# A scheduler's counts for a transpose through DRAM, and an SBUF margin 64 bytes wider, in a two-MoE kernel

## The chip, the cores and the metric

One core of a Trainium2 chip runs the whole program: TensorE (PE, with its weight loads shown apart as PEld), VectorE (DVE), ScalarE (ACT), GpSimd (POOL) and SyncE (SP), which here issues the transfers. The metric is the device time of one execution in microseconds, median of three. Less is better.

## The reference

Pooled attention, then an ELU mixture layer, then a second mixture layer with a softmax-gated linear unit and a layer norm. The change concerns the last of them:

```python
def _moe2_ref(x, w_in, w_out, g_ln):          # x: 4608 x 512, d_ff = 1024
    h = x @ w_in
    e = np.exp(h - np.max(h, axis=-1, keepdims=True))
    solu = h * (e / (np.sum(e, axis=-1, keepdims=True) + 1e-09))
    mu = np.mean(solu, axis=-1, keepdims=True)
    var = np.mean((solu - mu) ** 2, axis=-1, keepdims=True)
    ln = (solu - mu) / np.sqrt(var + 1e-06) * g_ln
    return (ln @ w_out).astype(np.float32)
```

## The kernel before

Attention and the first MoE fill the first 877 us of the execution. The second MoE follows. It works on 36 tiles of 128 tokens, in 18 pairs `n`; `tiles_of(n)` gives a pair's two tiles, called A (the first) and B (the second) here.

**The products of a pair.** `x @ w_in` is done by seven products P1, P2, S2, S1, S3, T4, S4 (`z_mul`, `prod`, L1008 to L1042), each of six matmuls with 512 columns. Numbers are split into a high and a low part. Seven weight tiles of 8192 bytes per partition are the moving operands. Three of them, B11 (product P1), B21 (P2) and T1 (S1), are written in place into the pool `pm` at SBUF's right edge. The other four, T2 (S2), T3 (S3), T4 (T4) and B22 (S4), are fetched from DRAM into the ring `w` of the pool `sb` on the left. In the compiled program of before, the `pm` tiles begin at bytes 204736, 212928 and 221120 of a partition, each 64 past a multiple of 128. The `sb` tiles (33536, 25344, 74496, 66304) begin on multiples of 128. The pool `edge`, one tile of 8 floats that nothing reads, lies to the right of `pm`. The scratch pool `pg` lies to the left of `pm`.

**The banks and their copies.** P1, S2, S3 and T4 add up in one bank X. ScalarE copies the bank out between them (`snap`, L1025: `p1` after P1, `u2` after S2, `u3` after S3). So S2 waits for the copy `p1`, with only P2 between, and S3 waits for `u2`, with only S1 between.

**A tile's way.** When its `h` stands: maximum (`max`, DVE L1066), exponential (`exp`, ACT L1072), product (`mul`, DVE L1076 to L1079), mean taken off (`sub`, ACT L1083), square (`sq`, ACT L1088), variance (`var`). Then the tile is transposed. In the first and the last pair TensorE does it (`pe`). In the other 16 pairs, 32 tiles, the tile goes through DRAM: a 32 by 32 transpose on DVE (`T`, L1102), a store to `zd` (`s`, L1107), four loads back into `dT` (`l`, L1114), the high part on ACT (`hi2`, L1122) and the low part on DVE (`lo2`, L1126). Then come 24 matmuls (`po`, L1153), the scaling on ACT (`st`, L1159) and the output store (L1160).

**The order.** TensorE's order is written out (`seq`): in a pair n, P1 P2 S2 S1 S3, then `po` of tile B of pair n-2, then T4 S4, then `po` of tile A of pair n-1. The orders on ACT, DVE and SP come from `arrange`, a list scheduler that runs when the program is built. Each operation has an engine, a duration `dur`, a latency `lat` after it, and dependencies. Working back from TensorE's wanted times it gives each operation a latest start. Going forward, it takes for each engine, among the operations that its own counts say are ready within 0.35 us of the first, the one with the earliest latest start. The engines then execute that order strictly. An operation whose data are late holds up all that stands behind it on its engine. SP also issues the loads of `x1r` (`xl`, L958, 1 MB for two pairs).

Of the kernel before, what the change touches and what calls it, by code (L numbers as in the profile page):

```python
# [8 lines left out]
F32 = mybir.dt.float32  # L9
# [11 lines left out]
def kernel(  # L21
# [16 lines left out]
    P = 128  # L38
# [63 lines left out]
    st = {}  # L102
# [1350 lines left out]
    for pr in range(NTP):  # L1453
# [11 lines left out]
        if last:  # L1465
            third.close()
            att.close()
            edge = ctx.enter_context(tc.tile_pool(name="edge", bufs=1, side="right"))
            edge.tile([P, 8], F32, name="edge")
            pm = ctx.enter_context(tc.tile_pool(name="pm", bufs=3, side="right", reuse_waits="tile"))  # L1470
            att2 = ExitStack()
            pg = att2.enter_context(tc.tile_pool(name="pg", bufs=2, side="right", reuse_waits="tile"))
# [35 lines left out]
        for s in range(7):  # L1508
            banks = o_banks(s)
            for t in range(4):  # L1510
                mul_o(s, t, banks, s in (0, 1, 2), s in (1, 5, 6))
                if s + 1 < 7:
                    for i in range(2):
                        w_ring(("o", s + 1, 2 * t + i))
                    n = ORDER[s + 1]
# [47 lines left out]
    def tiles_of(n):  # L1563

        c, q = divmod(n, 2)
        return 4 * c + q + 2, 4 * c + q
# [87 lines left out]
    tiles = [i for n in range(NPAIR) for i in tiles_of(n)]  # L1654
    outs = [i for key, i in seq if key == "po"]

    def op(key, eng, dur, deps, f=None, *a, lat=0.0, at=0.0):
        ops[key] = dict(eng=eng, dur=dur, deps=deps, lat=lat, at=at, f=f, a=a)
# [3 lines left out]
    for key, n in seq:  # L1662
        k = (key, n)
        if key == "po":
            j = outs.index(n)
# [17 lines left out]
    for n, (a, b) in enumerate(map(tiles_of, range(NPAIR))):  # L1683
        if n > 1:
            c = n // 2
            if n % 2 == 0 and c > 1:
                old = [(k, 2 * c - 3) for k in ("sums", "h0", "hi", "l0", "lo")] if c > 2 else []
                op(("xl", c), "SP", 0.55, old, p2_load, c, lat=5.0, at=20.0 if c == 2 else 0.0)
            x = [("xl", c) if c > 1 else "x1", ("S4", n - 2)]
            op(("open", n), None, 0.0, x, p2_open, n)  # L1690
            op(("sums", n), "DVE", 1.45, [("open", n), ("lo", n - 2), ("hi", n - 2)], p2_sums, n)
            op(("h0", n), "ACT", 0.95, [("open", n)], p2_hi, n, slice(0, 2))
            op(("hi", n), "ACT", 1.02, [("sums", n)], p2_hi, n, slice(2, 3))
            op(("l0", n), "DVE", 1.0, [("h0", n)], p2_lo, n, slice(0, 2))
            op(("lo", n), "DVE", 1.18, [("hi", n)], p2_lo, n, slice(2, 3))
        ha = ("s" if n > 2 else "sub", B_(max(n - 2, 0)) if n > 1 else None)
        hb = ("s" if n > 2 else "mul", A_(n - 1) if n > 2 else A_(0) if n == 2 else None)
        op(("p1", n), "ACT", 0.56, [("P1", n), ("ha0", n - 1)], snap, n, "p1", "X")
        op(("u2", n), "ACT", 0.56, [("S2", n), ("hb1", n - 1)], snap, n, "u2", "X")
        op(("u3", n), "ACT", 0.56, [("S3", n), ("ha0", n), ("ha1", n - 1)], snap, n, "u3", "X")  # L1700
        op(("ha0", n), "DVE", 0.62, [("P2", n), ("p1", n), ha], z_add, n, "ha0")
        op(("hb1", n), "DVE", 0.66, [("S1", n), ("u3", n), hb], z_add, n, "hb1")
        op(("hb0", n), "ACT", 0.57, [("T4", n), ("hb1", n)], z_add, n, "hb0")
        op(("ha1", n), "DVE", 0.66, [("S4", n), ("u2", n), ("ha0", n)], z_add, n, "ha1")
        for i, h, key in ((a, ("hb0", n), "b"), (b, ("ha1", n), "a")):
            j, jo = tiles.index(i), outs.index(i)
            e2 = [(k, tiles[j - 2]) for k in ("T", "pe", "sq")] if j > 1 else []
            op(("max", i), "DVE", 1.18, [h, ("hb1", n)] + ([("st", tiles[j - 6])] if j > 5 else []), s_max, i, n, key)
            op(("exp", i), "ACT", 1.3, [("max", i)] + e2, s_exp, i)
            op(("mul", i), "DVE", 1.75, [("exp", i)], s_mul, i)  # L1710
            op(("sub", i), "ACT", 1.12, [("mul", i)], s_sub, i)
            op(("sq", i), "ACT", 1.2, [("sub", i)], s_sq, i)
            op(("var", i), "DVE", 0.12, [("sq", i)], s_var, i, lat=0.9)
            free3 = [("po", outs[jo - 3])] if jo > 2 else []
            if n in (0, last):
                op(("hi2", i), "ACT", 1.08, [("pe", i)] + free3, t_ph, i)
                op(("lo2", i), "DVE", 1.3, [("hi2", i)], t_pl, i)
            else:
                op(("T", i), "DVE", 1.18, [("sub", i)], t_dve, i)
                op(("s", i), "SP", 0.4, [("T", i)], t_store, i, lat=2.4)  # L1720
                op(("l", i), "SP", 1.75, [("s", i)] + ([("lo2", tiles[j - 2])] if n > 1 else []), t_load, i, lat=2.1)
                op(("hi2", i), "ACT", 1.0, [("l", i)] + free3, t_hi, i)
                op(("lo2", i), "DVE", 1.2, [("hi2", i)], t_lo, i)
            op(("st", i), "ACT", 0.66, [("po", i), ("var", i)] + ([("os", outs[jo - 1])] if jo else []), z_store, i)
            op(("os", i), None, 0.0, [("st", i)], lat=2.4)
    for o in ops.values():
        o["deps"] = [d for d in o["deps"] if d in ops]
    with tc.manual_schedule():
# [38 lines left out]
```

## Time and profile before

| | us |
|---|---|
| median of 3 runs (1273.32 to 1275.31) | 1273.57 |
| profiled execution: its time | 1271.55 |
| profiled execution: span of the trace | 1269.4 |
| TensorE busy in the span | 1242.0 (98%) |
| VectorE / ScalarE busy | 984.8 (78%) / 824.0 (65%) |
| second MoE: first matmul to last | 877.1 to 1265.2 |

The busy shares are averages over three different stages. In a row of a timeline the first number is the start in us, the second the length, then engine, line, operation, tiles written and read, count, and in brackets the idle time just before it and what ended it. "sn" is the tile of the copies p1, u2 and u3, "zX" the bank X.

### The profile page before, as it was taken

Reading aid. Unit: us, or ns where it says so; the run is one execution under the profiler, and the core shown is the slowest. Engines: PE = TensorE matmul, PEld = TensorE weight load, DVE = VectorE, ACT = ScalarE, POOL = GpSimd, SP = SyncE. Lnnn points to the kernel's source line nnn. Section 1 sums busy time; section 2 is a strip of 40 time slices with the busy share of each in tenths; the row PEclk is TensorE's granted clock in tenths of the full one; section 3 lists DMA queues with packets and bytes.
Section 4 is the critical chain, followed back from the end, with each engine's and each line's share of the span. In section 5 each row is a group of like instructions: output and inputs, shape, how many; then the busy total and the mean of one; then the engine's idle time right before and its main releaser. Section 6 shows DMA issues by size and latency. Waiting matters only on the chain.

```text
span 1269.4 us, 17238 instructions
## 1 busy us (share of the span) xinstructions
PE 1242.0 (98%) x5768; PEld 993.9 (78%) x5768; DVE 984.8 (78%) x1484; ACT 824.0 (65%) x1405; POOL 177.7 (14%) x148
## 2 busy tenths in 40 slices
PE   8899999999999999999999999999998999999998
PEld 6777877777777878778888778888886878887777
DVE  8898687978877799676795778986886777778673
ACT  7887566666757784457764468743776667667564
POOL 4564222333210000100000000000000000000000
PEclk8999999999999999999999999999998999999999
DMA  9975366675768867787666888878454544544341
GB/s 323 296 218 191 125 220 221 214 234 168 237 205 274 252 214 243 222 294 199 203 215 201 287 254 270 288 256 306 151 172 141 158 140 143 169 147 141 108 143 57
DMA packets 177065, 263.30 MB, mean 207 GB/s; under 512 B 16465, under 2 KB 96849, under 8 KB 175953
## 3 DMA queue, kind: packets, MB, share of 16 engines
q1 hardware_dynamic: 176976, 262.21, 64.5%
q8 instruction: 46, 0.75, 0.2%
q14 instruction: 43, 0.34, 0.1%
HBM read 182.46 MB, written 79.69 MB: 207 GB/s over the span
## 4 chain that ended last, share of the span: by engine, by line
PE 64%; DVE 13%; DMA 13%; ACT 5%; issue 2%; SPq 2%; POOL 0%; ACTq 0%; DVEq 0%; POOLq 0%
PE hA L818 12%; PE oA L908 11%; PE o L694 9%; PE h L639 9%; PE po L1153 5%; DMA dT<-zd 4%; PE at L192 3%; PE oB L908 3%; PE zX L1015 3%; DMA zd<-ha 2%; PE at L277 2%; PE pt L251 2%; PE hB L818 2%; SPq L1114 2%; DVE e L1078 2%
## 5 line engine op out<-in xcount | busy, mean ns | idle before, releaser
L1153 PE MATMUL po<-w,dhl 128*128 128x512 f32 x864 | 203.7, 392 | 0.0
L908 PE MATMUL oA<-op,wr 128*128 128x512 f32 x864 | 202.4, 392 | 0.0
L908 PEld LDWEIGHTS oA<-op,wr 128*128 128x128 f32 x864 | 160.8, 188 | 38.1 <-issue 2.9
L1153 PEld LDWEIGHTS po<-w,dhl 128*128 128x128 f32 x864 | 162.1, 188 | 35.3
L898 ACT CAST op<-g 128x1024 fp32r<-128x1024 f32 x84 | 87.9, 1050 | 72.3 <-PE oA L908 33.3
L899 DVE TENSOR_TENSOR op<-g,op 128x1024 fp32r<-128x1024 f32 x84 | 102.8, 1230 | 34.1 <-ACT op L898 33.8
L818 PE MATMUL hA<-sS,wr 128*128 128x512 f32 x432 | 108.8, 394 | 1.5 <-ACT sp L830 1.5
L1015 PE MATMUL zX<-w,xh 128*128 128x512 f32 x288 | 102.8, 398 | 7.5 <-ACT sn L1025 7.4
L1093 POOL TENSOR_TENSOR sc<-sc,mhalf 128x1 f32<-128x1 f32 x36 | 21.1, 595 | 575.1 <-DVE sc L1092 300.1
L560 POOL TENSOR_TENSOR wol<-wo,woh 128x512 fp32r<-128x512 f32 x48 | 74.0, 1543 | 172.7 <-ACT woh L559 172.7
L818 PEld LDWEIGHTS hA<-sS,wr 128*128 128x128 f32 x432 | 79.9, 188 | 21.1 <-ACT sp L830 3.0
L241 POOL TENSOR_TENSOR es<-es,sm 128x720 f32<-128x720 f32 x28 | 48.2, 1720 | 305.7 <-DVE sm L239 137.3
L639 PE MATMUL h<-xh,wh 128*128 128x512 f32 x192 | 79.6, 415 | 2.4 <-DVE e L656 2.4
L694 PE MATMUL o<-gh,woh 128*128 128x512 f32 x192 | 77.5, 404 | 0.0
L838 DVE SCALAR_TENSOR_TENSOR g<-ep,g 128x512 f32<-128x512 f32 x72 | 50.9, 712 | 33.9 <-ACT ep L837 33.6
L639 PE MATMUL h<-xh,wl 128*128 128x512 f32 x192 | 76.2, 397 | 0.0
L639 PE MATMUL h<-xl,wh 128*128 128x512 f32 x192 | 76.0, 396 | 0.0
L694 PE MATMUL o<-gh,wol 128*128 128x512 f32 x192 | 75.1, 391 | 0.0
L1126 DVE TENSOR_TENSOR dhl<-dT,dhl 128x1024 fp32r<-128x1024 f32 x32 | 39.2, 1225 | 44.0 <-ACT dhl L1122 43.9
L1015 PEld LDWEIGHTS zX<-w,xh 128*128 128x128 f32 x288 | 54.7, 190 | 23.3 <-ACT sn L1025 11.0
L1122 ACT CAST dhl<-dT 128x1024 fp32r<-128x1024 f32 x32 | 33.6, 1049 | 46.9 <-DMA dT<-zd 46.8
L836 ACT ACTIVATE ep<-g 128x512 f32<-128x512 f32 x72 | 44.9, 628 | 26.2 <-DVE g L870 13.3
(354 smaller groups left out, 2759.8 us busy)
## 6 DMA issues: line engine op xcount, KB each, us to landing
wr<-w1d SPq DMA_DIRECT2D x168, 256.0 KB, 3.9
wr<-w3d SPq DMA_DIRECT2D x168, 256.0 KB, 3.0
raw<-in_w SPq DMA_DIRECT2D x48, 512.0 KB, 5.6
dT<-zd SPq DMA_DIRECT2D x128, 128.0 KB, 2.8
v<-in_v SPq DMA_DIRECT2D x32, 288.0 KB
x1r<-x1d SPq DMA_DIRECT2D x9, 1024.0 KB, 16.1
out<-ot SPq DMA_DIRECT2D x36, 256.0 KB, 3.7
w1d<-ci SPq DMA_DIRECT2D x16, 512.0 KB, 2.9
```

Source lines behind the costliest of these rows:

```text
L241: eng.tensor_tensor(es, es, bc(sm, n), op=ALU.mult)
L560: nc.gpsimd.tensor_tensor(ol, t[:, f % 4, :], oh.bitcast(F32), op=ALU.subtract)
L639: nc.tensor.matmul(h[:, 0:n], a[g][:, kk, fo:fo + P], x[j][:, kk, 0:n], start=(kk == 0 and m == 0), stop=(kk == KDM - 1 and m == 2), skip_ ...
L694: nc.tensor.matmul(acc, a[:, dm * P:(dm + 1) * P], x[:, 0:n], start=(f == 0 and m == 0), stop=(f == NF - 1 and m == 2))
L818: nc.tensor.matmul(bank, w[:, a, kk], x[:, b, kk], start=(start and m == 0), stop=(stop and m == 5), skip_group_check=True,)
L836: nc.scalar.activation(e, h, AF.Relu, scale=-1.0)
L838: gate["dve"] = nc.vector.scalar_tensor_tensor(d, e, 1.0, h, op0=ALU.subtract, op1=ALU.max).ins
L898: gate["act"] = nc.scalar.copy(o[:, 0], src).ins
L899: gate["dve"] = nc.vector.tensor_tensor(o[:, 1], src, o[:, 0].bitcast(F32), op=ALU.subtract).ins
L908: nc.tensor.matmul(banks[d], ws[i][:, a, d * P:(d + 1) * P], o[:, b, i], start=(start and t == 0 and i == 0 and m == 0), stop=(stop and t ...
L1015: nc.tensor.matmul(bank, x[:, o:o + P], w[:, y + k, :], start=(start and m == 0), stop=(stop and m == 5), skip_group_check=True,)
L1153: nc.tensor.matmul(po, a[:, c], b[c // 4][:, c % 4, :], start=(m == 0), stop=(m == 3 * NC2 - 1))
```

## The change

Four numbers change. The margin `edge` becomes 24 floats wide. In the scheduler's table the latency of the store `s` becomes 3.0 us, that of the loads `l` 4.0 us, and that of the output store `os` 3.5 us.

```diff
-            edge.tile([P, 8], F32, name="edge")
+            edge.tile([P, 24], F32, name="edge")
@@ for each tile of pairs 1 to 16
-                op(("s", i), "SP", 0.4, [("T", i)], t_store, i, lat=2.4)
-                op(("l", i), "SP", 1.75, [("s", i)] + ([("lo2", tiles[j - 2])] if n > 1 else []), t_load, i, lat=2.1)
+                op(("s", i), "SP", 0.4, [("T", i)], t_store, i, lat=3.0)
+                op(("l", i), "SP", 1.75, [("s", i)] + ([("lo2", tiles[j - 2])] if n > 1 else []), t_load, i, lat=4.0)
                 op(("hi2", i), "ACT", 1.0, [("l", i)] + free3, t_hi, i)
                 op(("lo2", i), "DVE", 1.2, [("hi2", i)], t_lo, i)
             op(("st", i), "ACT", 0.66, [("po", i), ("var", i)] + ([("os", outs[jo - 1])] if jo else []), z_store, i)
-            op(("os", i), None, 0.0, [("st", i)], lat=2.4)
+            op(("os", i), None, 0.0, [("st", i)], lat=3.5)
```

Pools hand out space in steps of 64 bytes here, so everything that lies to the left of the margin on the right side, the three tiles of `pm` and the scratch of `pg`, moves 64 bytes lower. The `pm` tiles then begin at 204672, 212864 and 221056, multiples of 128, though not of 256. No instruction is added or taken away; the scheduler may give ACT, DVE and SP another order in the second MoE.

## Rows read from the trace of the kernel before

**Rows 1.** The page: its first line, and TensorE's busy time and share.

```profile
span 1269.4 us, 17238 instructions
PE 1242.0 (98%) x5768; PEld 993.9 (78%) x5768; DVE 984.8 (78%) x1484; ACT 824.0 (65%) x1405; POOL 177.7 (14%) x148
```

**Rows 2.** Who waited, 876 to 1270: total us, times, longest us.

```profile
ACT dhl L1122 <- DMA dT<-zd: 46.8, 28, 4.2
PE zX L1015 <- ACT sn L1025: 7.4, 6, 4.1
```

**Rows 3.** Timeline of TensorE, 966.3 to 982.

```profile
966.41 0.39 PE L1015 MATMUL zX<-w,xh 128*128 128x512 f32 x1
967.81 0.39 PE L1015 MATMUL zY<-w,xh 128*128 128x512 f32 x1
...
973.50 0.79 PE L1015 MATMUL zX<-w,xh 128*128 128x512 f32 x1 [4.12 <-ACT sn L1025]
...
978.78 0.43 PE L1015 MATMUL zX<-w,xh 128*128 128x512 f32 x1
```

**Rows 4.** Stretch 975 to 980: busy us by engine, granted clock, DMA share, GB/s.

```profile
975.00:980.00 5.00, 5.00 (x16) 3.91 (x15) 3.88 (x11) 2.83 (x5) 0.00 (x0) 0.62 0.62 192
```

**Rows 5.** Timeline of ScalarE, 960 to 975.

```profile
969.69 1.04 ACT L1122 CAST dhl<-dT 128x1024 fp32r<-128x1024 f32 x1 [4.17 <-DMA dT<-zd]
970.64 1.14 ACT L1083 ACTIVATE e<-e,sc 128x1024 f32<-128x1024 f32 x1
...
972.88 0.57 ACT L1025 COPY sn<-zX 128x512 f32<-128x512 f32 x1
```

**Rows 6.** Timeline of SP's transfers, 960 to 975.

```profile
960.02 0.38 SPq L1107 DMA_DIRECT2D zd<-ha  x1
960.46 0.54 SPq L958 DMA_DIRECT2D x1r<-x1d  x1
963.29 1.74 SPq L1114 DMA_DIRECT2D dT<-zd  x4
```

**Rows 7.** Timeline of TensorE, 1140 to 1150: the second longest of the six waits.

```profile
1144.91 0.50 PE L1015 MATMUL zX<-w,xh 128*128 128x512 f32 x1 [1.54 <-ACT sn L1025]
```

**Rows 8.** Timelines of DVE and ACT: shortest and longest ways from `T` to `hi2`.

```profile
1078.03 1.25 DVE L1102 STREAM_TRANSPOSE hb<-e 128x1024 f32<-128x1024 f32 x1
1086.20 1.05 ACT L1122 CAST dhl<-dT 128x1024 fp32r<-128x1024 f32 x1 [0.47 <-DMA dT<-zd]
...
1189.54 1.24 DVE L1102 STREAM_TRANSPOSE ha<-e 128x1024 f32<-128x1024 f32 x1
1201.38 1.05 ACT L1122 CAST dhl<-dT 128x1024 fp32r<-128x1024 f32 x1 [2.56 <-DMA dT<-zd]
```

**Rows 9.** Lines L1107 (stores), then L1114 (loads): us from issue to landing.

```profile
DMA to landing us min/median/max: 2.8/2.9/5.4
...
DMA to landing us min/median/max: 2.2/2.8/5.3
```

**Rows 10.** Timelines of DVE and PE: least and most time from `lo2` to `po`.

```profile
1197.07 1.23 DVE L1126 TENSOR_TENSOR dhl<-dT,dhl 128x1024 fp32r<-128x1024 f32 x1 [2.51 <-ACT dhl L1122]
1199.39 2.00 PE L1153 MATMUL po<-w,dhl 128*128 128x512 f32 x8
...
982.30 1.23 DVE L1126 TENSOR_TENSOR dhl<-dT,dhl 128x1024 fp32r<-128x1024 f32 x1 [0.58 <-ACT dhl L1122]
988.44 1.77 PE L1153 MATMUL po<-w,dhl 128*128 128x512 f32 x7
```

**Rows 11.** Timeline of TensorE, 924 to 958: starts of products with weights from `sb`.

```profile
930.65 0.39 PE L1015 MATMUL zX<-w,xh 128*128 128x512 f32 x1
...
932.03 5.66 PE L1153 MATMUL po<-w,dhl 128*128 128x512 f32 x24
937.53 0.39 PE L1015 MATMUL zX<-w,xh 128*128 128x512 f32 x1
...
938.89 0.39 PE L1015 MATMUL zZ<-w,xh 128*128 128x512 f32 x1
```

## The prediction

> **What bounds the kernel now.** I read the page first, then who waited for whom in the second MoE, then the timelines around each wait. The page shows TensorE busy for 1242.0 of 1269.4 us [rows 1], so the end moves only with TensorE: by its idle time, by its clock, or by the spacing of its matmuls. The table of waits shows where it stands idle in this stage: six times, 7.4 us in all, always the same way [rows 2]. The product S2 waits for ScalarE's copy p1 of bank X. The same table names what ScalarE waits for: 28 times, 46.8 us in all, for `dT` to land [rows 2].
>
> The longest case shows how the two hang together. S2 starts at 973.50, after 4.12 us of idling [rows 3]. The copy it wants starts at 972.88. Ahead of it on ScalarE stand `hi2`, which waited 4.17 us for its load, and `sub`, which ran right behind [rows 5]. P1, whose bank p1 copies, had been done since before 968. So ScalarE sat on a late transpose with ready work queued behind it. The loads were late because a 1 MB load of `x1r` had been issued between the store and the loads [rows 6]. Each of the six waits has a `hi2` that waited for `dT` some 3 to 9 us ahead of its copy.
>
> **The table's counts, step by step.** From the end of `T` to the start of `hi2` the scheduler before counts 0.4 + 2.4 (store) + 1.75 + 2.1 (loads) + 3 x 0.06 (its gap between engines) = 6.83 us. I took the real time for all 32 tiles from the starts of L1102 and L1122. The shortest is 1086.20 - 1079.28 = 6.92, the longest 1201.38 - 1190.78 = 10.60 [rows 8], the median 7.74. All 32 are above the count. After the change the count is 9.33, and 26 of 32 are below it. The order of before was therefore made for a transpose that never comes so early. The new order puts up to 2.5 us of other work, above all `sub` and `sq` (1.1 us each, the former in [rows 5]), ahead of `hi2`, and `lo2` and whatever DVE has behind it move with it.
>
> *What the six waits cost.* Idle: 7.4 us [rows 2]. Clock: after the longest wait the granted clock is 0.62 of full over 975 to 980 [rows 4], a mix of the 1.2 and the 2.4 GHz level. TensorE had idled 4.12 us just before. Twelve matmuls go from 973.50 to 978.78, 5.28 us, where two undisturbed products take 2 x (967.81 - 966.41) = 2.80 [rows 3]: 2.5 us. Restart: the first matmul after a shorter wait lasts 0.50 [rows 7] against 0.39 [rows 3], 0.1 each, five times: 0.5 us. Together 10.4 us, the most that this part can give.
>
> *What remains of them.* Six tiles exceed 9.33, by 0.34 to 1.28 us, 3.3 us in all. Some of that excess comes from lateness that was passed on: a late `hi2` delays the next tile's `sub` and `T`. I take 1.5 us as left over, between 0 and 3.3. Gain: 8.9 us.
>
> *The wait that the change adds.* A `hi2` that is later in the order makes `lo2` later, and `po` waits for `lo2`. Behind a waiting `po` stands all of TensorE. Today `po` never waits. For tile A of a pair the time from the end of `lo2` to `po` is 1.10 us at least (1199.39 - 1198.30) and 4.91 at most (988.44 - 983.53) [rows 10]; the 16 values are 1.10, 1.41, 1.55, 1.61, 2.07, 2.41, 2.46, 3.01, 3.11, 3.23, 3.40, 3.64, 4.19, 4.26, 4.31 and 4.91. If every `hi2` really slips behind `sub` and `sq` by 2.3 us, five tiles fall short, by 1.20 + 0.89 + 0.75 + 0.69 + 0.23 = 3.8 us. The scheduler sees this chain and has room left for nearly all, and where `dT` lands early and ScalarE is idle, `hi2` starts early all the same. Between 0 and 3.8 I take 1.5. For tile B the room is larger, 2.6 us and up.
>
> *SP.* Each `l` is four issues, 1.74 us [rows 6], and waits on SP for its store to land, with output stores, the next `s` and `x1r` queued behind. Counted 0.6 us later, it lets those go first more often. Their landing matters only in this way to the same `hi2`, so it is in the 1.5 us left over. *The output store.* Its 3.5 for 2.4 binds two successive `st`, which are over 5 us apart since a `po` of 5.5 us lies between: nothing.
>
> *One rule to weigh here.* The landing times are 2.9 us in the median for stores and 2.8 for loads, with 5.4 and 5.3 at most [rows 9]. The Trainium skill, "DMA: Bandwidth & Descriptors", section "Anatomy of one DMA", gives a DMA a nearly constant cost of about 2.0 us plus bytes over bandwidth. By that rule the old counts were about right and the new ones only hold `hi2` back, so this part would give a loss of up to the 3.8 us above. The medians here are 0.8 us and more above that fixed cost and the tails 3.3 us above, so I go by the rows.
>
> **The margin.** The three `pm` tiles begin 64 bytes past a multiple of 128 and after the change on one. P1, with one of them, takes 967.81 - 966.41 = 1.40 us [rows 3]. S3, with a tile of `sb`, which starts on a multiple of 128, takes 932.03 - 930.65 = 1.38, and T4 takes 938.89 - 937.53 = 1.36 [rows 11]. All have six matmuls of 512 columns. Over the stage, the 324 matmuls on `pm` tiles start 0.233 us apart in the median, those of T4 and S4 0.227, and those of S2 and S3 between. The step follows the place of the moving tile, but two things differ together, the step of 64 bytes and the far right region, and no row parts them. With 3 products x 18 pairs = 54, an alignment as good as T4's gives 54 x 0.04 = 2.2 us, one like S3's 54 x 0.02 = 1.1. If the region is the cause, 0. Nothing excludes that the new place is worse; by the same step the other way it costs 1.1. I take 1.6, halfway between the two aligned rows. `pg`, moved too, holds scratch of a few DVE and ACT instructions: nothing. The moves change no transfer.
>
> **The sum.** 8.9 - 1.5 + 1.6 = 9.0 us. The profiled execution took 1271.55 us, its span 1269.4 and 2.15 around it; it becomes 1262.6. It lies 2.0 below the median of the runs, so from the median 1273.57 I forecast **1264.6**.
>
> **Rivals.** *(a) The margin buys nothing*, because the region and not the 64 bytes sets the spacing. For it: no other moving tile lies so far right. Then 1273.57 - 7.4 = 1266.2. A rule points the same way. The Trainium skill, "TensorE: Matmul & The Clock Gate", section "Back-to-back issue gap", has the gap depend on the number of columns and the clock only. The trace disagrees at equal columns and full clock (0.233 against 0.227 us), so it gets less than half.
>
> *(b) The waits stay.* The loads that collide with `x1r` are late by more than any count, and `hi2` stays just ahead of p1 in the new order too. Then only the margin shows, 1273.57 - 1.6 = 1272.0, within 0.2%. For it: the longest way is 10.60, above 9.33. Against it: most of the 28 waits had no `x1r` near them.
>
> *(c) Slower: `po` waits for `lo2`.* In the A tiles `hi2` slips behind `sub` and `sq`, and then `lo2`, in order on DVE, slips behind a `mul` or `max` too. With a slip of D the 16 waits sum to what D exceeds the 16 times above: 3.8 us at 2.3, 12 us at 3.4, 22 us at 4.25 (2.5 counted plus the 1.75 of a `mul`). From D of about 3.4 on it eats the 10.4 + 1.6 us gained. At 4.25 the time is 1273.57 - 12.0 + 22.1 = 1283.7. For it: ACT and DVE are busy 65 and 78% [rows 1], so slots are scarce. Against it: the scheduler gives `hi2` and `lo2` an earlier latest start exactly where the room is small.
>
> **How the numbers follow.** Forecast 0.48, (a) 0.24, (b) 0.16, (c) 0.12. The range goes from all waits gone and T4's spacing, 1273.57 - 10.4 - 2.2 = 1261.0, up to 1272.5, which takes in (b) and both bounds of the left-over and added waits. It leaves out (c) and a little on either side. About 0.2%, 2.5 us, is what a measurement of this kernel can tell from no change. Forecast and (a) are faster by more, (b) is within, (c) is slower: 0.72, 0.16, 0.12.
>
> **What would show it.** Right: ScalarE's wait for `dT` falls from 46.8 us to under 20, the wait of zX for sn from 7.4 to under 2, no stretch of the stage has a granted clock below 1.0, and P1, P2 and S1 take 1.36 to 1.38 us. Wrong: `po` waiting for `lo2`; zX still waiting for sn behind a late `hi2`; products on `pm` tiles still at 1.40; or a new wait for a copy with `sub` or `exp` just ahead of it, which I have not priced.

## The result, and the profile after

The changed kernel took 1258.13 us (median of 4 runs, 1256.80 to 1263.21) against 1274.17 (4 runs of the kernel before): a ratio of 0.9881, interval 0.9852 to 0.9910. Timed again later, 5 runs against 23 of the kernel before, it took 1261.09 against 1272.85: 0.9900, interval 0.9884 to 0.9917. So it is faster by about 1.0 to 1.2%, some 12 to 16 us, where 9.0 was forecast. The forecast 1264.6 had the direction right, and the part of the kernel where the gain lies. The first measurement lies 2.9 us below the range's low end of 1261.0, the second 0.1 us above it.

The profiled execution took 1263.21 us, its span is 1261.4. From the first matmul of line 1015 to the last one of all, the second MoE takes 375.7 us (881.8 to 1257.5) where it took 388.3 (877.1 to 1265.4). The table of waits in this stage, in the columns of [rows 2], shows why:

```profile
ACT sn L1025 <- PE zX L1015: 45.2, 47, 2.2
...
DVE dhl L1126 <- ACT dhl L1122: 5.9, 7, 1.8
ACT dhl L1122 <- DMA dT<-zd: 3.8, 4, 2.0
```

ScalarE's wait for `dT` is down from 46.8 us to 3.8 [rows 2], and there is no row any more of zX waiting for sn. ScalarE now waits for TensorE's bank (45.2 us, first row): as a rule ScalarE is free for the copy when the product ends. The place of the longest wait [rows 3, 5, 6] looks like this, on ScalarE first:

```profile
968.86 1.15 ACT L1083 ACTIVATE e<-e,sc 128x1024 f32<-128x1024 f32 x1 [0.55 <-DVE sc L1079]
969.91 1.03 ACT L1122 CAST dhl<-dT 128x1024 fp32r<-128x1024 f32 x1
972.18 0.69 ACT L1159 ACTIVATE ot<-po,sc 128x512 f32<-128x512 f32 x1 [1.23 <-DMA out<-ot]
972.76 0.58 ACT L1025 COPY sn<-zX 128x512 f32<-128x512 f32 x1
```

`sub` (L1083) now stands ahead of `hi2` (L1122), which starts without any idle time. On SP the order is turned too, the four loads go ahead of the 1 MB load:

```profile
960.23 0.38 SPq L1107 DMA_DIRECT2D zd<-ha  x1
963.03 1.74 SPq L1114 DMA_DIRECT2D dT<-zd  x4
964.88 0.53 SPq L958 DMA_DIRECT2D x1r<-x1d  x1
```

TensorE's products there follow each other:

```profile
970.39 0.40 PE L1015 MATMUL zX<-w,xh 128*128 128x512 f32 x1
...
971.78 0.40 PE L1015 MATMUL zY<-w,xh 128*128 128x512 f32 x1
...
973.39 0.50 PE L1015 MATMUL zX<-w,xh 128*128 128x512 f32 x1
```

From P1's first matmul to S2's it is 3.00 us, against 7.09 in [rows 3]. Two undisturbed products take 2.80 [rows 3], so 0.2 us are still lost here: the copy stood behind the scaling (L1159), which had waited 1.23 us for an output store. So short a wait of TensorE is in no row of the table. The granted clock of the two stretches after it is full (columns as in [rows 4]):

```profile
970.00:975.00 5.00, 4.95 (x22) 3.72 (x21) 4.96 (x7) 2.11 (x4) 0.00 (x0) 1.00 0.34 120
975.00:980.00 5.00, 5.00 (x24) 4.07 (x23) 3.95 (x12) 3.46 (x5) 0.00 (x0) 1.00 0.56 176
```

### The profile page after: what moved, and what is told of

Same layout as the page of the kernel before. It is cut to its first block, busy times and chain, and to the rows that moved or that the text cites. A ratio compares the mean times of both kernels' runs of the same rounds, so it can differ in the third digit from the quotient of the medians.

```text
span 1261.4 us, 17236 instructions
## 1 busy us (share of the span) xinstructions
PE 1236.6 (98%) x5768; PEld 992.7 (79%) x5768; DVE 986.4 (78%) x1484; ACT 822.3 (65%) x1405; POOL 177.3 (14%) x148
## 4 chain that ended last, share of the span: by engine, by line
PE 83%; DVE 8%; DMA 5%; ACT 2%; issue 2%; POOL 0%; SPq 0%; DVEq 0%; ACTq 0%; POOLq 0%
PE po L1153 15%; PE oA L908 14%; PE hA L818 13%; PE zX L1015 8%; PE o L694 7%; PE h L639 7%; PE zZ L1015 4%; PE at L192 3%; PE oB L908 3%; PE hB L818 2%; PE zY L1015 2%; PE at L277 2%; PE pt L251 2%; DMA x0d<-xr 1%; DMA sP<-x0d 1%
## 5 line engine op out<-in xcount | busy, mean ns | idle before, releaser
L908 PE MATMUL oA<-op,wr 128*128 128x512 f32 x864 | 202.4, 392 | 0.0
L908 PEld LDWEIGHTS oA<-op,wr 128*128 128x128 f32 x864 | 160.8, 188 | 38.0 <-issue 2.9
L818 PE MATMUL hA<-sS,wr 128*128 128x512 f32 x432 | 108.7, 393 | 2.2 <-ACT sp L830 2.2
L818 PEld LDWEIGHTS hA<-sS,wr 128*128 128x128 f32 x432 | 79.9, 188 | 21.7 <-ACT sp L830 3.6
L892 DVE TENSOR_TENSOR g<-g,g 128x1024 f32<-128x1024 f32 x48 | 61.3, 1291 | 0.1
L1025 ACT COPY sn<-zX 128x512 f32<-128x512 f32 x54 | 31.7, 587 | 45.5 <-PE zX L1015 45.2
```

Source lines behind the costliest of these rows:

```text
L818: nc.tensor.matmul(bank, w[:, a, kk], x[:, b, kk], start=(start and m == 0), stop=(stop and m == 5), skip_group_check=True,)
L892: nc.vector.tensor_tensor(d, x, y, op=op)
L908: nc.tensor.matmul(banks[d], ws[i][:, a, d * P:(d + 1) * P], o[:, b, i], start=(start and t == 0 and i == 0 and m == 0), stop=(stop and t ...
```

## The experiments

The theory: the scheduler counted the way from `T` to `hi2` shorter than it ever is, `hi2` was put into ScalarE's order too early, and held up the copy that S2 wants. The rivals: any other order would do; the gain is an accident of the first two profiles; the margin carries a good part; the new order on SP brings the tiles back sooner.

**Both kernels again, and each part alone.** `before_again` and `after_again` are the two kernels unchanged. `counts_only` is the changed kernel with

```diff
-            edge.tile([P, 24], F32, name="edge")
+            edge.tile([P, 8], F32, name="edge")
```

and `margin_only` the kernel before with the opposite edit.

> The kernel before, timed against itself. Theory 1 (the profile of before was one typical execution, the missing 3.4 us of the gain lie in the other stages and differ from run to run): the ratio is 1.000 within 0.002, and in this second profile the second MoE takes about 388 us again (377 to 1265) with zX waiting for sn by 5 to 9 us, while the stages ahead of it differ by up to 4 us from the first profile. Theory 2 (the profile of before was a lucky one in the second MoE itself): the second MoE takes 390 us or more here, with more than 10 us of waiting for sn or a second stretch at a lower granted clock.

> The changed kernel again. Theory 1: ratio 0.987 to 0.989, the second MoE takes 375 to 377 us in this profile too, without any wait of zX for sn, and the 4.5 us by which the first MoE was longer in the first profile of it (514.5 against 510.0 us) are not there. Theory 2 (the first MoE is really longer with the change): it takes 514 us again.

> The three counts of the change, the margin at 8 floats as before. Theory 1 (all of the gain comes from the order): second MoE within 0.5 us of the changed kernel's 375.7, no wait of zX for sn, P1, P2 and S1 at 1.400 us each; ratio within 0.001 of the changed kernel's. Rival (the margin carries 1.6 us or more, as forecast): second MoE 377 us or more.

> The margin of the change, 24 floats, with the counts of before. Theory 1 (the margin buys next to nothing): second MoE within 1 us of 388, the six waits of zX for sn as in before, P1 at 1.391 and S1 at 1.392 instead of 1.400; ratio 0.999 to 1.001. Rival (the 64 bytes give 1.6 us or more): ratio under 0.9985, and P1, P2 and S1 at 1.37 or less.

| run | ratio, interval | first MoE's L818 to L908 part, us | second MoE, us |
|---|---|---|---|
| before_again | 0.9989, 0.9971 to 1.0008 | 509.5 | 386.5 |
| after_again | 0.9900, 0.9884 to 0.9917 | 511.9 | 376.2 |
| counts_only | 0.9898, 0.9881 to 0.9914 | 511.4 | 376.6 |
| margin_only | 0.9994, 0.9982 to 1.0006 | 510.5 | 388.1 |

(The third column runs from the last matmul of line 694 to the first of line 1015.) The counts are the whole gain that can be measured, and the margin alone makes no measurable difference. The stage of `counts_only` is 0.9 us longer than that of the first profile of the changed kernel, where 0.5 was expected, and 0.4 longer than that of the second. The rows of `counts_only` and of `margin_only`:

```profile
ACT dhl L1122 <- DMA dT<-zd: 3.5, 3, 2.0
```

```profile
ACT dhl L1122 <- DMA dT<-zd: 50.3, 28, 3.8
...
PE zX L1015 <- ACT sn L1025: 7.9, 7, 3.7
```

The expectation for `after_again` missed in part: the ratio is 0.9900, just above the 0.987 to 0.989, one wait of zX for sn of 0.2 us is there, and the first MoE's part, which nothing in the change touches, took 511.9 us here and 514.5 in the first profile, against 509.5 to 510.5 in three profiles with the counts of before. With `counts_only` it was 511.4, in the runs below 508.5 to 511.5. So it scatters by some 6 us. That the kernel before itself ran between 1268.03 and 1276.99 in 23 runs fits that.

**Which count.** Three kernels with one count raised or lowered, all with the margin of before:

```diff
# os_only
-            op(("os", i), None, 0.0, [("st", i)], lat=2.4)
+            op(("os", i), None, 0.0, [("st", i)], lat=3.5)
# stores_only
-                op(("s", i), "SP", 0.4, [("T", i)], t_store, i, lat=2.4)
+                op(("s", i), "SP", 0.4, [("T", i)], t_store, i, lat=3.0)
# loads_only (lat=4.0) and loads_less (lat=0.2), in the line of "l"
-                ... t_load, i, lat=2.1)
+                ... t_load, i, lat=4.0)
```

> Only the output store's count goes from 2.4 to 3.5; the margin and the counts of s and l as before. It gives ACT and DVE another order too. Theory 1 (the gain comes from counting the transpose's way as long as it is): the way is still counted 6.83 us, so ScalarE goes on waiting 35 us or more for dT, zX waits 4 to 10 us for sn, the second MoE takes 384 to 390 us, ratio 0.997 to 1.001. Rival (any other order gets rid of these six waits): second MoE under 380 us, ratio 0.993 or less.

> Only the store's count goes from 2.4 to 3.0. The way is counted 7.43 us, more than 14 of the 32 real ways of the kernel before took. Theory 1: the wait of ScalarE for dT falls to between 15 and 40 us, zX waits 2 to 7 us for sn, second MoE 380 to 387 us. Rival (the store is the late part, so that its count does all): second MoE 376 to 378 us.

> Only the loads' count goes from 2.1 to 4.0. The way is counted 8.73 us, more than 25 of the 32 real ways. Theory 1: ScalarE waits under 10 us for dT, zX under 1.5 us for sn, second MoE 376 to 379 us, ratio 0.989 to 0.993. Rival (s or os is needed): second MoE 382 us or more.

> The other direction: the loads' count goes from 2.1 down to 0.2, the way is counted 4.93 us, below all real ones by 2 us and more. Theory 1: ScalarE waits 60 us or more for dT, zX more than 10 us for sn, second MoE 392 us or more, ratio 1.003 or more. Rival (the counts matter only by chance of the order): second MoE within 3 us of before's 387.

Their rows of the table of waits, first `os_only`:

```profile
ACT dhl L1122 <- DMA dT<-zd: 50.1, 24, 5.3
...
PE zX L1015 <- ACT sn L1025: 11.8, 5, 4.0
```

`stores_only`:

```profile
ACT dhl L1122 <- DMA dT<-zd: 33.5, 20, 3.2
...
PE zX L1015 <- ACT sn L1025: 6.9, 3, 4.9
```

`loads_only`:

```profile
ACT dhl L1122 <- DMA dT<-zd: 7.5, 6, 2.6
PE zX L1015 <- ACT sn L1025: 0.3, 1, 0.3
```

`loads_less`:

```profile
ACT dhl L1122 <- DMA dT<-zd: 85.9, 31, 8.6
...
PE zX L1015 <- ACT sn L1025: 29.5, 11, 6.9
...
PE po L1153 <- ACT dhl L1122: 1.0, 1, 1.0
PE po L1153 <- DVE dhl L1126: 0.8, 1, 0.8
```

**The dose further.** `double_raise` is the changed kernel with s 3.6 and l 5.9. `counts_as_measured` is the kernel before with s 2.9, l 2.8 and os 3.7, the medians of the landing times [rows 9] and of the output store's (3.7 on the page).

> Twice the raise: s 3.6, l 5.9, os 3.5, margin 24. The way is counted 11.83 us, above every real way of before. Theory 1 with a price on the other side: ScalarE waits under 2 us for dT, but the scheduler now plans a lag of TensorE itself (its own end of the chain is 6.9 us later than with the counts of before), lo2 comes too late for po in some tiles A, and PE waits 2 to 8 us in all for lo2 or for a copy; second MoE 378 to 385 us, ratio 0.992 to 0.998. Rival (more room is only better or neutral): second MoE 375 to 377 us, ratio 0.988 to 0.991.

> The counts set to the medians of the trace of before: s 2.9, l 2.8, os 3.7, margin 8. The way is counted 8.03 us, more than about 20 of the 32 real ways. Theory 1 (it is the share of ways that come later than counted that costs): between the run with only the store's count (7.43) and the one with only the loads' (8.73): ScalarE waits 8 to 30 us for dT, zX 0.5 to 5 us for sn, second MoE 377 to 384 us. Rival (a count at the median does as well as one above most): second MoE within 1 us of 376.

| run | way counted, us | ACT waits for dT, us | zX waits for sn, us | second MoE, us | ratio, interval |
|---|---|---|---|---|---|
| loads_less | 4.93 | 85.9 | 29.5 | 426.6 | 1.0281, 1.0247 to 1.0315 |
| before | 6.83 | 46.8 | 7.4 | 388.3 | 1 |
| os_only | 6.83 | 50.1 | 11.8 | 395.7 | 1.0043, 1.0025 to 1.0062 |
| stores_only | 7.43 | 33.5 | 6.9 | 386.0 | 0.9959, 0.9940 to 0.9978 |
| counts_as_measured | 8.03 | 7.6 | 2.1 | 379.0 | 0.9934, 0.9914 to 0.9954 |
| loads_only | 8.73 | 7.5 | 0.3 | 377.0 | 0.9900, 0.9860 to 0.9940 |
| after_again | 9.33 | 3.7 | 0.2 | 376.2 | 0.9900, 0.9884 to 0.9917 |
| double_raise | 11.83 | none | none | 379.3 | 0.9936, 0.9912 to 0.9961 |

Ordered by the way counted, ScalarE's wait falls almost step by step, and the stage with it, down to the changed kernel. In `counts_as_measured` the wait of 7.6 us is just under the 8 to 30 expected. `os_only` decides against "any other order will do": its order on ACT and DVE is another one, the way is counted as in before, and the wait for `dT` stays. It is slower, against my expectation of no difference, because two of its waits are long, 4.01 and 3.73 us, and TensorE stood at half its full clock, the 1.2 GHz level, right after each:

```profile
1017.00:1022.00 5.00, 4.97 (x12) 3.90 (x13) 4.86 (x14) 2.95 (x4) 0.00 (x0) 0.50 0.61 206
1022.00:1027.00 5.00, 5.00 (x22) 4.08 (x21) 3.26 (x4) 3.00 (x4) 0.00 (x0) 0.95 0.49 165
1065.00:1070.00 5.00, 5.00 (x12) 3.93 (x13) 4.86 (x14) 2.96 (x4) 0.00 (x0) 0.50 0.63 210
```

By the starts of the products these two waits with the slow stretches behind them cost 13.2 us, where before had one such wait for 6.8.

`double_raise` shows the other side, the rival (c) of the prediction in small. Its row for line 1153, TensorE with its weight loads, under "its engine sat idle before it until":

```profile
  DVE dhl L1126: 4.8, 14
```

Fourteen times TensorE waits there for `lo2`; by the starts these `po` lose 0.15 to 0.5 us each, 3.0 us in all; ScalarE waits for no `dT` at all. The best of the counts tried lie between the median of the way of before and its longest. Nothing here beats the changed kernel clearly: its products lose 0.85 us in all, measured as spacing above each product's median.

**Back no sooner, used later.** The counts turn SP's order too, and no run has one order without the other. The traces speak against the rival that the tiles merely come back sooner. In the changed kernel the first load of a tile is issued a median 3.47 us after the end of `T`, against 2.93 before, and `hi2` starts 9.32 us after it, against 7.74. The times from issue to landing of the loads, in the changed kernel and in `counts_as_measured`:

```profile
DMA to landing us min/median/max: 2.3/2.7/3.8
...
DMA to landing us min/median/max: 2.2/2.7/5.8
```

The median is that of before [rows 9] within 0.1 us. The longest fell in the changed kernel, from 5.3 to 3.8, but in `counts_as_measured` it is 5.8, longer than before, and ScalarE still waits for `dT` only 7.6 us. So the gain comes in the main from the later place of `hi2`; what SP's order adds was not measured by itself.

**The margin.** `margin_40` is the changed kernel with 40 floats. `left_shift` has 64 bytes put in at the left edge:

```diff
# margin_40
-            edge.tile([P, 24], F32, name="edge")
+            edge.tile([P, 40], F32, name="edge")
# left_shift
+    cst.tile([P, 16], F32, name="pad")
     ident = cst.tile([P, P], F32, name="ident")
```

> The changed kernel with a margin of 40 floats, which puts the three weight tiles another 64 bytes lower, 64 past a multiple of 128 as in before. Theory (the step of 64 bytes sets the spacing, whatever the region): P1 and S1 go from 1.392 back to 1.400 us with all six matmuls 0.233 apart; second MoE longer by 0.3 to 0.5 us, not to be seen in the total. Rival (the region sets it): P1 and S1 stay at 1.392 with spacings that alternate.

> The changed kernel with 64 bytes put in at the left edge of SBUF, so that every tile of the left side, all other moving operands of the two MoEs among them, begins 64 past a multiple of 128. If the step of 64 bytes alone sets the spacing of 0.233 us: T4 and S4 go from 1.36 to 1.40, S2 and S3 from 1.375 to 1.40, a po from 5.49 to 5.59, the second MoE is longer by about 6 us and the first by about 10, ratio about 1.003. If it is the far right region: nothing changes, T4 and S4 stay at 1.36, ratio 0.988 to 0.992.

Neither expectation held. The starts of T4 and S4 of pair 6, in `after`, in `margin_40` and in `left_shift` (its lines are one further down):

```profile
1003.79 0.39 PE L1015 MATMUL zX<-w,xh 128*128 128x512 f32 x1
...
1005.15 0.39 PE L1015 MATMUL zZ<-w,xh 128*128 128x512 f32 x1
```

```profile
1001.36 0.40 PE L1015 MATMUL zX<-w,xh 128*128 128x512 f32 x1
...
1002.74 0.39 PE L1015 MATMUL zZ<-w,xh 128*128 128x512 f32 x1
```

```profile
998.86 0.40 PE L1016 MATMUL zX<-w,xh 128*128 128x512 f32 x1
...
1000.24 0.39 PE L1016 MATMUL zZ<-w,xh 128*128 128x512 f32 x1
```

T4 takes 1.36 us, 1.38 and 1.38. Its weights, from `sb`, did not move at all in `margin_40`, nor did its other operand, and its bank is the same. The medians over 18 pairs:

| us per product | P1 | P2 | S2 | S1 | S3 | T4 | S4 |
|---|---|---|---|---|---|---|---|
| counts_only (margin of before) | 1.400 | 1.400 | 1.380 | 1.400 | 1.379 | 1.360 | 1.359 |
| after | 1.391 | 1.400 | 1.375 | 1.392 | 1.374 | 1.360 | 1.359 |
| margin_40 | 1.390 | 1.373 | 1.389 | 1.384 | 1.390 | 1.381 | 1.359 |
| left_shift | 1.390 | 1.373 | 1.389 | 1.384 | 1.390 | 1.381 | 1.359 |

The last two rows are equal to the thousandth, though in one the `pm` tiles begin 64 past a multiple of 128 and in the other on one, and the left tiles the other way round. What the two share is the distance between the `pm` tiles and the left side: 171072 bytes from T2 to B11, against 171136 in after and 171200 in before. The seven add up to 9.68, 9.65, 9.67 and 9.67 us, so over 18 pairs all four lie within 0.5 us. The totals cannot tell them apart: 0.9917 (0.9892 to 0.9942) for `margin_40`, 0.9912 (0.9890 to 0.9935) for `left_shift`.

## Why the prediction was wrong in size and right in cause

**The count and the order: right.** The way was counted too short, and the six waits and the slow clock went with it. The table above moves with the counted way in both directions.

**What the six waits cost: too small.** I summed 7.4 idle, 2.5 clock and 0.5 restart to 10.4. By the starts, which is how TensorE's time passes, the products of before lose 12.25 us above their medians: 8.6 between P2 and S2, 1.9 in S2 and 1.25 in S1 (both mostly the clock), 0.5 elsewhere. S2's median is itself lifted by short waits, 1.42 us against 1.38 in `counts_only`, 0.7 us over 18 pairs. Together 13.0. The idle time in the table is counted from the modelled end of the last matmul, which lies some 0.16 us after the point where the next could have begun: matmuls of 0.39 us start 0.23 apart. From 968.98, the start of P2's last matmul, to 973.50 it is 4.52 us, so 4.29 were lost there, not 4.12. And waits shorter than that overlap are in no row.

**What remains: too much.** I left 1.5 us, because six real ways were longer than 9.33. In the changed kernel the products lose 0.85 us, about half of it not from these waits. That some of the long ways were themselves carried over from earlier late ones was in the prediction, but only 1.8 of 3.3 us were taken off for it. In the longest case SP's new order, with the 1 MB load behind the four loads, took the collision away too.

**The wait that was to be added: there is none.** I charged 1.5 us because a later `hi2` makes `lo2` later. The step that failed is the assumption that the rest of the tile's way stays where it was. What moves ahead of `hi2` is the `sub` of the next tile, so that tile's `T` starts earlier. For tile A of pair 14, which had the least room [rows 10], before:

```profile
1175.34 0.39 PE L1015 MATMUL zX<-w,xh 128*128 128x512 f32 x1
...
1186.88 1.23 DVE L1102 STREAM_TRANSPOSE hb<-e 128x1024 f32<-128x1024 f32 x1
```

and after:

```profile
1168.91 0.39 PE L1015 MATMUL zX<-w,xh 128*128 128x512 f32 x1
...
1176.75 1.25 DVE L1102 STREAM_TRANSPOSE hb<-e 128x1024 f32<-128x1024 f32 x1 [1.22 <-ACT e L1083]
1187.94 1.18 DVE L1126 TENSOR_TENSOR dhl<-dT,dhl 128x1024 fp32r<-128x1024 f32 x1
1192.27 1.08 PE L1153 MATMUL po<-w,dhl 128*128 128x512 f32 x4
```

`T` starts 7.84 us after the first matmul of T4 instead of 11.54. `hi2` comes later after `T` than before (8.21 us after its end instead of 7.87), and still `lo2` ends 3.15 us ahead of `po` instead of 1.10. Over the 16 pairs the median from T4's end to `T`'s end falls from 9.34 to 7.58, and the median room of tile A is 2.92 against 3.06. The least is 0.54 against 1.10, still enough.

**The margin: mis-sized, and for a wrong reason.** I took 1.6 us from the spacing of single products and asked whether the step of 64 bytes or the region sets it. Neither does by itself, as `margin_40` and `left_shift` show. P1, P2 and S1 went to 1.391, 1.400 and 1.392, not to the 1.36 to 1.38 named as the sign of being right. It gave 0.03 us per pair (9.68 to 9.65 in the table), 0.5 us over 18 pairs, and no total shows it. Rival (a), which said it buys nothing, was nearer.

**The output store: not nothing.** I put its count at nothing, because two successive `st` are far apart. `os_only` shows that this count alone turns the orders on ACT and DVE, and its stage took 395.7 us instead of 388.3. In the whole change it does no visible harm: `loads_only`, without it, has 377.0 and the changed kernel 375.7 and 376.2.

**The rule on DMA cost.** The Trainium skill, "DMA: Bandwidth & Descriptors", section "Anatomy of one DMA", gives its nearly constant 2.0 us, plus bytes over 436 GB/s, as a fit for transfers that GpSimd issues; here SyncE issues them. The prediction's step from there to "the old counts were about right" left out the bytes. By that fit of the Trainium skill, as an estimate, a store of 512 KB takes 3.2 us, a load of 128 KB 2.3, and the way about 7.8 us, well above the old count. The trace has 2.9 and 2.8 in the median [rows 9] and a way of 7.74, so the rule did not speak for the old counts. `counts_as_measured`, with the medians of this trace, beats the old counts (0.9934). The longer counts of `loads_only` leave shorter waits still, 0.3 us of zX for sn instead of 2.1, and a stage of 377.0 us instead of 379.0. Their totals are not apart: the intervals of 0.9900 and 0.9934 overlap.

**The range.** The waits were priced 2.6 us too low, left over and added wait together 2.15 too high (3.0 for 0.85), the margin 1.1 too high: 9.0 + 2.6 + 2.15 - 1.1 is about 12.6, and 12.6 was measured in the stage between the first two profiles (10.3 between the second two). The low end stood on the total of three runs within 2 us. The later 23 runs spread over 9 us, by the profiles mostly from stages that the change doesn't touch (6 us in the first MoE's part, 2 us between the two profiles of before in the second MoE). An honest low end was the full recovery, 1261.0, less half of that spread. Of the 16 us between the first two medians some 12 are the stage's; that the rest is scatter is argued from those 23 runs and the second timing, not shown run by run.

## What to carry to other kernels

Where a list scheduler writes an order that engines follow strictly, a latency counted short costs far more than one counted long: here 1.9 us less cost 2.8%, 2.5 us more won 1.0%, and 5 us more gave about a third of that back (0.9936 against 0.9900, with intervals that just overlap; the stage shows it, 379.3 us against 376.2). Set such a count above most of the measured ways, from the end of the producer to the start of the consumer in the trace, not at the median landing time. When pricing a wait on TensorE, count from start to start, and when something is put ahead of a late operation, ask what that something starts early.

## What the runs showed of the hardware

The time of a product with the same six matmuls varies between 1.359 and 1.400 us with where tiles lie in SBUF. Moving the three right tiles by 64 bytes changed T4, whose own weights did not move, from 1.360 to 1.381, and moving everything on the left by 64 bytes instead gave the same seven times to the thousandth. Whether a tile begins on a multiple of 128 bytes showed no effect of its own: it is the other way round in those two runs with equal times, and with all left tiles 64 past one the first MoE's part took 508.5 us against 509.3 to 514.5 in the other runs. What in the distance matters is open; it wasn't tried further. The Trainium skill, "TensorE: Matmul & The Clock Gate", section "Back-to-back issue gap", gives the gap of an isolated matmul by columns and clock alone, and says that in a stream with weight loads both set the spacing; where the tiles lie is no term of either. The trace shows a difference that neither has: these products, each matmul with its own weight load, differ by 3% at equal columns and full clock.
